# One tile more on split operands: the sixth tile's theta and the sixth step of the first mixing, in an attention and mixing kernel on one core

## The chip, the cores and the metric

The kernel runs on one core of a Trainium2 chip. The metric is device time in microseconds (us), taken from the start of the program to its end; a kernel is run several times and the median is shown. A profile is taken of one execution. Its span is the time between the first and the last instruction that the profiler saw, and the execution's own time is a little longer.

The core has five engines that run their own instruction queues in order and wait for each other through semaphores: TensorE (PE: matmuls, with its weight loads shown apart as PEld), VectorE (DVE), ScalarE (ACT), GpSimd (POOL), and SyncE (SP), which here issues every DMA.

## The reference, cut to what matters

Inputs: q, k and v of shape (4, 8, 768, 64), and four weight matrices. First a local attention with block summaries:

```python
k_sum = k.reshape(B, H, nb, 32, D).max(axis=3)
v_sum = v.reshape(B, H, nb, 32, D).mean(axis=3)
# scores of the keys within 16 positions, and of the 24 block summaries (+ log 32); one softmax over both
a = softmax([masked q k^T, q k_sum^T + log 32]);  attn = a @ [v, v_sum]
```

Then x is the attention's output as (4, 768, 512), and

```python
theta = x @ w_theta                                   # 512 x 512
zr, zi = x * cos(theta), x * sin(theta)
y = einsum('ts,bsd->btd', w_tok_r, zr) + einsum('ts,bsd->btd', w_tok_i, zi)   # 768 x 768 each
u = x + y
out = u + max(u @ w_ch, 0)
```

The weights come as 64-bit floats and are turned into 32-bit floats on the chip. All matrix products have to be good to 32-bit floats.

## The kernel before, in words

**Tiles and stages.** A batch has 768 positions, cut into six tiles of 128 positions. There are 24 tiles in all, numbered through; tiles 0 to 5 are batch 0, so "the sixth tile" is tile 5. For each tile the kernel computes the attention (`att_tile` L454: scores L490, masking with the row maximum on DVE L526, exponentials on ACT L530, transposes L539 with their copies L543, products with v L513, normalising L553 to L560); transposes the result (`turn_tile` L564: transposes L569, copy into x); computes theta and its sine and cosine (`theta_tile` L589); and multiplies to zr and zi (L631). The theta PSUM tile, `t`, has one buffer, and the transposes of `turn_tile` use the same one.

**Mixing.** For each batch there are two mixings, one for each half of the 512 channels (`mix_step` L641). One mixing has six steps, one for each tile; a step multiplies the tile's zr and zi (the stationary operands, two pieces of 128 channels each) with the rows of w_tok_r and w_tok_i that belong to the tile, and adds up in PSUM. After the sixth step DVE adds the sums to x (L678).

**The last stage.** When all batches are mixed, the channel product with w_ch is done by `out_batch` (products L775), in a scheme of seven products of half size, with sums and differences formed by DVE and POOL.

**Whole and split operands.** There are two ways to make a product that is good to 32 bits:

- whole: one matmul on 32-bit operands; the profile shows two records for it.
- split: each operand is cut into a high part in the reduced type `F32R` (`hi_op`, L289, a copy with conversion) and a low part (`lo_op`, L298, the difference), and three matmuls are made: high by high, high by low, low by high.

Two numbers decide which tiles go which way. A theta whose tile number is below `RT` is made on whole operands (L594), any other on split ones (L599). A step of the first mixing whose tile number is below `RM` is whole, any other split; the second mixing of batch 0 and all later ones are split. Both are 6 before.

```python
            if b * NT + i < K["RT"]:                                   # L593, theta_tile
        raw = b * NT + i < K["RM"]                                     # L625, theta_tile
        if t < K["RM"]:                                                # L896, after mix_step t
            for j in (2 * s, 2 * s + 1):
                split_wt(j, f_t[j])
        if j < 2 * K["RM"]:                                            # L876, weight piece j of 12
```

On split operands a tile's x is copied three times out of PSUM: whole into x, high into `xh`, low into `xl` (L571 to L577); on whole ones, once. Its z is split by `split_z` (L582). The theta weights are split (`split_f64`, L394) right ahead of the first theta that needs them. The mixing weights come in 12 pieces, j = 0 to 11, two for each step; each is turned into 32-bit floats by `to_f32` (L367 to L389, ACT, POOL and DVE). A piece of a whole step is kept as a 32-bit float, and is split after that step for the second mixing. A piece with j at or above 2 x `RM` is split at once, out of the buffer `f` (two buffers) that the conversion works in; the loads of the next batch's v (`prepass`, L435 to L440) use the same two.

**What sets the order.** Nothing is planned when the program is built: every operation (a group of instructions on one engine) has a number, in the order in which the functions register them, and the text `ORDER` lists the numbers in the order in which they are issued. A letter behind a number names the engine where several could do the work (a ScalarE, d VectorE, g GpSimd). `schedule` (L222) only reads the list. Each engine works off its own operations in that order, so an instruction that waits holds up all that stand behind it on its engine. Where DVE and POOL share work, POOL's instruction is made to wait for the DVE instruction listed just before it (the end of `attn_moe`).

## Time and profile before

| | us |
|---|---|
| median of 3 runs | 453.76 (452.31 to 454.28) |
| the profiled execution | 452.55 |
| its span | 450.8 |
| PE busy | 439.6 |
| DVE busy | 327.9 |
| ACT busy | 275.3 |
| POOL busy | 114.3 |

How to read it: a line of the profile names the source line, the engine, the operation, and the tiles it writes and reads (`m<-wt,zh` writes the mixing sums `m` and reads weights and the high part of z). Whole mixing products stand under L659 like split ones. In the chain of waits each piece has its start, its length and what it is; a piece "x24" has 24 records. In a timeline row, square brackets hold how long the engine was idle before it and what released it. A window's row gives each engine's busy time in that stretch.

### The profile page before, as it was taken

What the parts mean: (1) busy time and instruction counts of PE and PEld (TensorE: products, weight loads), DVE (VectorE), ACT (ScalarE), POOL (GpSimd) and SP (SyncE); (2) the same over time, 40 slices, a digit from 0 to 9 for tenths busy, and PEclk for the clock granted to TensorE, in tenths of its full rate; (3) what the DMA queues carried; (4) which work ended last, traced back from release to release, by engine and by line L of the source; (5) the groups of instructions that cost most, each with busy time, mean ns of one, the idle gap of its engine ahead of it and who ended that gap; (6) DMA issues with size and microseconds to landing.
All of it is one profiled execution on the core that took longest, in us unless ns stands there. A gap on an engine that the chain in (4) does not pass through costs nothing.

```text
span 450.8 us, 9379 instructions
## 1 busy us (share of the span) xinstructions
PE 439.6 (98%) x3562; PEld 358.9 (80%) x3562; DVE 327.9 (73%) x919; ACT 275.3 (61%) x579; POOL 114.3 (25%) x126
## 2 busy tenths in 40 slices
PE   7889999999999999999999999999999999999996
PEld 3455655667888888888888888888888878999996
DVE  5899999579657964666745365735646599999896
ACT  2899997787665658746684666757873123434130
POOL 3332204844251130050210100112011310114652
PEclk9999999999999999999999999999999999999999
DMA  8999965222165530405323040102005700002138
GB/s 289 358 355 333 353 185 164 90 82 70 59 224 179 151 102 22 131 19 163 101 78 106 3 117 25 55 1 76 4 0 190 278 1 0 1 1 72 53 138 300
DMA packets 24573, 55.53 MB, mean 123 GB/s; under 512 B 2768, under 2 KB 7888, under 8 KB 24528
## 3 DMA queue, kind: packets, MB, share of 16 engines
q1 hardware_dynamic: 24528, 54.93, 37.3%
q8 instruction: 28, 0.46, 0.4%
q14 instruction: 17, 0.14, 0.1%
HBM read 45.48 MB, written 9.44 MB: 122 GB/s over the span
## 4 chain that ended last, share of the span: by engine, by line
PE 90%; DMA 7%; SPq 1%; ACT 1%; DVE 0%; issue 0%; ACTq 0%
PE m L659 46%; PE t L599 11%; PE c L775 7%; PE m L775 6%; PE pa L513 5%; PE s L490 4%; PE pa L539 4%; PE t L594 3%; DMA wt<-wtr 3%; PE t L569 3%; DMA wth<-wth 2%; DMA q<-qg 2%; SPq L286 1%; PE t L775 1%; PE pa L443 0%; ACT vs L446 0%
## 5 line engine op out<-in xcount | busy, mean ns | idle before, releaser
L659 PE MATMUL m<-wt,zh 128*128 128x512 f32 (+1 forms) x768 | 179.4, 359 | 0.6 <-DVE x L678 0.6
L659 PEld LDWEIGHTS m<-wt,zh 128*128 128x128 f32 x768 | 124.0, 188 | 31.8 <-issue 12.8
L659 PE MATMUL m<-wt,zl 128*128 128x512 f32 x336 | 86.4, 338 | 0.0
L530 ACT ACTIVATE e<-e,st 128x118 f32<-128x118 f32 x192 | 62.8, 387 | 8.1 <-DVE st L526 7.6
L659 PEld LDWEIGHTS m<-wt,zl 128*128 128x128 f32 x336 | 51.5, 188 | 7.6
L526 DVE CUSTOM_DVE_ANT_0 e<-s,cs 128x118 f32<-128x118 f32 x192 | 44.4, 273 | 5.2 <-PE s L490 4.2
L599 PE MATMUL t<-wth,xh 128*128 128x512 f32 x144 | 46.7, 406 | 0.0
L610 DVE SCALAR_TENSOR_TENSOR w<-w,t 128x512 f32<-128x512 f32 x24 | 16.4, 685 | 28.5 <-ACT w L608 28.4
L301 POOL TENSOR_TENSOR zl<-zb,zh 128x512 fp32r<-128x512 f32 x16 | 21.2, 1328 | 52.5 <-DVE zh L294 24.1
L473 POOL COPY k<-kn 128x376 f32<-128x376 f32 (+1 forms) x29 | 14.0, 492 | 80.6 <-DVE zl L301 43.2
L608 ACT ACTIVATE w<-t,bmagic 128x512 f32<-128x512 f32 x24 | 16.5, 688 | 23.5 <-PE t L599 21.4
L599 PE MATMUL t<-wth,xl 128*128 128x512 f32 x72 | 28.4, 395 | 0.0
L513 PEld LDWEIGHTS pa<-v,e 118*64 118x64 f32 x768 | 24.5, 137 | 4.7 <-issue 2.5
L513 PE MATMUL pa<-v,e 118*64 118x65 f32 x768 | 27.9, 224 | 0.1
L539 PEld LDWEIGHTS pa<-cs,e 128*118 128x118 f32 x192 | 22.1, 136 | 6.3 <-issue 1.9
L490 PE MATMUL s<-k,q 64*64 64x118 f32 x768 | 25.0, 268 | 1.8 <-POOL k L473 1.8
L539 PE MATMUL pa<-cs,e 128*118 128x128 f32 x192 | 26.1, 274 | 0.3 <-ACT vs L446 0.2
L543 ACT COPY e<-pa 118x512 f32<-118x512 f32 x35 | 19.5, 586 | 10.3 <-PE pa L539 10.2
L490 PEld LDWEIGHTS s<-k,q 64*64 64x64 f32 x768 | 19.5, 132 | 7.8 <-issue 3.6
L678 DVE TENSOR_TENSOR x<-m,x 128x512 f32<-128x512 f32 (+1 forms) x32 | 16.5, 551 | 12.6 <-PE m L659 12.4
L599 PEld LDWEIGHTS t<-wth,xh 128*128 128x128 f32 x144 | 22.6, 189 | 3.4 <-issue 0.2
L543 DVE COPY e<-pa 118x512 f32<-118x512 f32 x13 | 8.9, 687 | 21.0 <-PE pa L539 21.0
(173 smaller groups left out, 790.3 us busy)
## 6 DMA issues: line engine op xcount, KB each, us to landing
v<-vg SPq DMA_DIRECT2D x48, 195.0 KB, 4.0
q<-qg SPq DMA_DIRECT2D x24, 256.0 KB, 4.4
kn<-kT SPq DMA_DIRECT2D x6, 798.0 KB, 7.6
wt<-wtr SPq DMA_DIRECT2D x6, 768.0 KB, 11.7
wt<-wti SPq DMA_DIRECT2D x6, 768.0 KB, 12.2
f<-vT SPq DMA_DIRECT2D x12, 384.0 KB, 3.9
cu<-u_scratch SPq DMA_DIRECT2D x8, 384.0 KB, 6.4
out<-cu SPq DMA_DIRECT2D x16, 192.0 KB, 2.5
```

Source lines behind the costliest of these rows:

```text
L301: lambda e: V[e].tensor_tensor(dst(), src(), hi().bitcast(F32), op=ALU.subtract), reads, writes, due, port=BOTH)
L490: mm(0.79 * len(pairs) / NP, [lambda p=p, g=g, h=h: nc.tensor.matmul(sc[h].get()[ROW[g], p], q.get()[ROW[h], p, ROW[g]], k.get()[ROW[h], p ...
L513: mm(2 * 0.433 + scores[0] + (0.2 if scores[0] else 0.0), [lambda n=n, g=g, a=a: nc.tensor.matmul(xa[a].get()[ROW[g], n], turned[a].get()[ ...
L526: op({"DVE": 0.205}, lambda eng, n=n: nc.vector.tensor_tensor_reduce(e()[:, n], sc[n % 2].get()[:, 2 * a + n // 2], mask(m), -SCALE, 3.0e3 ...
L530: op({"ACT": 0.288}, lambda eng, n=n: nc.scalar.activation(e()[:, n], e()[:, n], AF.Exp, bias=st.get()[:, n:n + 1], scale=-1.0), [(st, n)] ...
L539: mm(NH * 0.109, [lambda n=n: nc.tensor.transpose(tp.get()[:NK, n], e()[:, n], ident()) for n in range(NH)], [e_ref, (cs, "ident")], [tp], ...
L543: lambda e: (nc.scalar.copy if e == "ACT" else nc.vector.tensor_copy)(t.get()[:NK], tp.get()[:NK].rearrange("k n q -> k (n q)")), [tp], [t ...
L599: calls = [lambda t=t, xx=xx, k=k, c=c: nc.tensor.matmul(th.get(), xx.get()[:, c], w_th[c].get()[:, k], start=(c == 0 and t == 0), stop=(c ...
L608: op({"ACT": 0.59}, lambda e: nc.scalar.activation(r(), th.get(), AF.Identity, bias=bmagic.get(), scale=1.0), [th, bmagic], [R], due)
L659: nc.tensor.matmul(acc[th](), zz.get()[:, r, cc], w[:, TT[th]], start=(s == 0 and r == 0 and t == 0 and (th == 0 or c == 0)), stop=(s == N ...
L678: op({"DVE": c_dve(nt * P)}, lambda e, u=u, acc=acc: nc.vector.tensor_tensor(u(), acc(), u(), op=ALU.add), [areg] + [(xs, n) for n in rang ...
L775: calls = [lambda k=k, t=t, x=x, y=y: nc.tensor.matmul(to.get(), weights[n][x][0]()[:, k, j * P:(j + 1) * P], operands[n].get()[:, y, k], ...
```

## The change

`RT` and `RM` go from 6 to 5. So the sixth tile's theta is made on split operands instead of whole ones, and so is the sixth step of batch 0's first mixing. The weight pieces j = 10 and 11 are split as soon as they are converted, instead of being kept whole and split after the sixth step; the theta weights' split is registered ahead of the sixth tile's theta instead of the seventh's. The sixth tile gets its high and low parts of x and of z: four operations more, 1976 instead of 1972, and with them the numbers in the list shift.

The list `ORDER` is new throughout: the order of operations on all engines differs, and many operations have another engine than before. Counted over the program, DVE has 728 operations instead of 727, ACT 487 instead of 473, POOL 111 instead of 122, PE 476 and SP 174 as before.

```diff
 ORDER = """
-23 0d 11d 17g 8d 9 25 29 27 39 31 33 86 18 19 20 21 24 1d 2 3 4 5 26 30 44a 48g 49a 46a 45g 50 28 47g 51 6d 7d 52 53 60 62
+23 25 0d 1d 27 29 39 17d 15 16 2 3 4 5 31 33 86 18 19 20 21 11d 8d 9 10 14 6d 7d 24 26 44g 45g 49g 28 30 47g 46a 48a 50 51
...
-            A1=13, T1=10, PREP=5, QB=2, VSPE=1, VB=4, KB=1, WARM=5, SP0=1, FUSE=99, RELOAD=2, RT=6, RM=6, XA=6, XB=2, ZB=4, ZS=6, EB=3, TAU_A=8.2, TAU_M=4,
+            A1=13, T1=10, PREP=5, QB=2, VSPE=1, VB=4, KB=1, WARM=5, SP0=1, FUSE=99, RELOAD=2, RT=5, RM=5, XA=6, XB=2, ZB=4, ZS=6, EB=3, TAU_A=8.2, TAU_M=4,
```

More of the change, by code (lines that the diff above doesn't have):

```diff
@@ new lines @@
+52 56 189g 188g 12 60 62 55 63 53 61 54 58 87a 64 65 57 59 66 67 35 79 80a 32 34 36 37 70 68 40 183 42 93 230 100 184 186
+190 88d 38d 13 89 90 91 92g 81d 82 83 41d 84 43a 69a 71a 233a 72 191 194 193 192 199 200 201 202 73d 76d 74 77 75d 78d 22
+195 198 94a 196 204 203 197 205 206 185g 187g 234g 95g 85g 235 101a 107 283 232 231 108 109 110 111 336 96 97 102g 207 209
+218 208a 210a 236 239 287a 219a 98 103 104 238 105 211 99a 237 244 212a 118a 213 246 247 215d 243 242 250 241 245 249 248
+240 216 214d 217d 251 106g 119g 286g 120 121 220 221 222 223 252 254 224 253a 255a 288 256 285 284 225 112 404 338 337 113
@@ new lines @@
+1270 1289 1232d 1208g 1234a 1235 1271 1272a 1236a 1317 1290 1293 1255 1297 1320a 1318a 1239d 1298 1256a 1257g 1344g 1284g
+1273 1292 1296 1300 1304 1345a 1237 1238d 1301 1319 1291 1274 1275 1240 1241d 1276d 1299 1294 1295 1305 1302 1303 1261 1279
+1321 1280 1322 1333 1334 1281 1323 1308 1306 1324 1307d 1309d 1335 1346 1310 1325 1326 1327a 1328 1347 1277d 1474 1329 1331d
+1475a 1311d 1312 1332g 1477a 1476 1336 1349 1355 1358 1356 1360 1359 1348 1352 1357 1313d 1330 1337 1339 1338 1478 1340 1376
@@ new lines @@
+1479 1377 1378 1379 1374a 1384d 1314a 1350 1315 1393a 1375g 1385g 1423a 1424d 1354 1316a 1351 1394a 1353 1361 1362 1381
+1429d 1430g 1383 1380 1480 1365 1363 1481 1482 1364a 1366d 1386 1342 1390 1391 1392 1343 1435 1395 1367 1483 1529 1396 1399
+1371d 1382 1398 1404 1407 1439a 1438a 1484a 1532a 1530a 1372 1406 1531 1405 1402 1368a 1387 1388 1533 1425 1389 1534 1427
+1369 1397 1370d 1401 1403 1400 1373a 1411 1409 1410 1408 1485 1535 1412 1414 1536 1426 1440 1468d 1413d 1415d 1537 1416 1538
+1539d 1441 1449 1553 1445 1451 1443 1469d 1447 1556a 1420d 1417a 1554a 1486 1555 1428 1433 1431 1557 1434 1442 1418 1421
@@ new lines @@
+1525a 1528d 1571 1589 1613 1572 1591 1616a 1614a 1615 1617 1618 1592 1619 1611 1620 1585 1587d 1590 1609 1612 1610 1588d
+1631 1632 1629 1630 1603a 1604 1605 1607d 1608g 1633 1634 1635 1636 1586 1606 1621 1622 1623d 1624 1625 1627a 1626 1628d
+1639 1640 1641 1637d 1638d 1647d 1648d 1642 1685 1698 1686 1704 1728 1731 1692 1792 1730 1793 1795 1729 1794 1687a 1705a
+1699d 1700d 1701 1702 1688d 1706d 1689 1707 1703 1708 1690 1693a 1694g 1643 1646 1644 1709 1645 1653d 1695 1696 1697 1691
+1654d 1720a 1659a 1710d 1714a 1715d 1649 1650 1651 1652 1657 1658 1655 1663 1656 1661 1662 1660d 1667 1664 1669 1670 1665a
@@ new lines @@
+1787 1840 1818a 1820a 1836a 1857d 1813d 1811d 1824 1874 1828 1863a 1865a 1838 1839d 1845 1895 1825 1841d 1869g 1864g 1846
+1853 1849 1832 1822 1842 1826 1829 1875a 1867a 1870a 1872a 1916a 1861d 1868d 1830 1833 1866d 1876 1879 1843 1854 1897 1917g
+1850 1955 1881 1877 1878a 1884 1934 1900 1847 1880a 1871d 1896a 1851 1918d 1898 1919d 1920a 1922d 1923a 1899a 1885 1873d
+1888 1902 1901a 1909 1892 1921d 1935a 1886 1925a 1905 1926d 1882 1893 1910 1906 1936 1889 1924g 1929g 1913 1939 1941 1927a
+1937 1928d 1890 1938a 1944 1960 1903 1914 1957 1907 1834 1827 1852 1791 1767 1788 1883 1855 1780 1759 1831 1894 1784 1887
```

126 lines of the change are left out of this document (51 added, 75 removed).

## The prediction

> **What bounds the kernel now.** The page comes first: its span, the busy shares and the slices.
>
> ```profile
> span 450.8 us, 9379 instructions
> PE 439.6 (98%) x3562; PEld 358.9 (80%) x3562; DVE 327.9 (73%) x919; ACT 275.3 (61%) x579; POOL 114.3 (25%) x126
> PE   7889999999999999999999999999999999999996
> PEclk9999999999999999999999999999999999999999
> ```
>
> TensorE (PE) works in 439.6 of 450.8 us, at the full granted clock, and it is the least busy in the first three slices and the last. So the time is PE's work plus 11.2 us in which it stands still. Second, the view of waits says who held PE:
>
> ```profile
> PE t L356 <- POOL zb L354: 1.8, 1, 1.8
> PE s L490 <- POOL k L473: 1.8, 2, 1.1
> PE t L569 <- DVE w L610: 1.2, 2, 0.6
> PE t L594 <- ACT x L292: 0.8, 1, 0.8
> PE t L594 <- DVE xn L560: 0.6, 1, 0.6
> PE m L659 <- DVE x L678: 0.6, 1, 0.6
> ```
>
> The first row is the start of the program. The others come to 5.0 us, and any order could at best win these back. Third, the windows show how close the other engines are (PE, PEld, DVE, ACT, POOL, clock, DMA share):
>
> ```profile
> 40.00:80.00 40.00, 39.87 (x213) 23.22 (x214) 39.48 (x88) 36.18 (x67) 10.27 (x12) 1.00 0.75 247
> 80.00:100.00 20.00, 19.13 (x253) 13.49 (x252) 12.43 (x60) 16.19 (x38) 13.85 (x20) 1.00 0.26 78
> 363.00:448.00 85.00, 84.00 (x479) 80.43 (x479) 79.05 (x128) 27.64 (x44) 24.83 (x15) 1.00 0.20 71
> ```
>
> From 40 to 80 us VectorE (DVE) is as full as PE: 39.48 of 40 against 39.87. There two engines bound the kernel together. From 80 to 100 DVE has 7.6 us to spare, and in the last stage 5.9 of 85. The change is made inside the first two windows.
>
> **The change part by part.** *PE's own work.* The chain of waits lists PE's pieces in order (start, length, what):
>
> ```profile
> 69.59 11.75 PE m L659 x36
> ...
> 89.08 0.93 PE t L594 x2
> ...
> 91.09 2.79 PE t L594 x6
> ...
> 98.07 3.02 PE t L599 x12
> 101.09 5.16 PE m L659 x16
> ...
> 113.78 1.05 PE m L659 x6
> 114.83 0.70 PE t L599 x3
> 115.53 3.12 PE m L659 x18
> ...
> 219.33 4.23 PE m L659 x24
> ```
>
> The sixth tile's theta on whole operands is the two L594 pieces, 0.93 + 2.79 = 3.72 us. On split operands a tile's theta is the L599 row with 12 records, 3.02 us. That saves 0.70. The sixth mixing step on whole operands is the 5.16 us row (16 records); a split step is 24 records, 4.23 us. That saves 0.93. Together **-1.63 us**.
>
> By the Trainium skill (FP8 and Floating Point Precision, section TensorE Precision Notes) a true fp32 product goes through the array in four passes. If each of the three split products were one such pass, my estimate from the page would be three quarters of 3.72 and of 5.16, a saving of 2.2 us. The rows give ratios of 0.81 and 0.82, so the rows decide.
>
> *Changes between kinds of matmul.* Counted along the two written orders, PE changes kind (products of the mixings, the channel stage and whole-operand theta; theta on split operands; scores; transposes; attention products) 245 times instead of 231. Changes between the first two sorts go from 91 to 107, all others from 140 to 138. Between these two a change costs next to nothing: six records of a split step take 1.05 between two theta pieces, and 18 without a break 3.12, which is 1.04 for six. Sixteen times 0.01 is 0.2, and two of the others fall away; I take 0, with +-0.3 as bounds.
>
> *The transposes of the seventh tile.* They reuse the PSUM tile of the sixth theta, so they wait for ScalarE's rounding and DVE's subtraction of it. The timeline:
>
> ```profile
> 95.36 0.66 PE L569 MATMUL t<-cs,xn 128*128 128x128 f32 x4 [0.63 <-DVE w L610]
> ...
> 97.03 1.04 PE L490 MATMUL s<-k,q 64*64 64x118 f32 x32
> ```
>
> Between the theta and them stood only eight transposes of the attention, and PE lost 0.63. In the new order a whole block of scores (about 1 us, last row) stands there too, which is more than was missing: **-0.6 us**. (A similar wait at the third tile goes, and another of its size appears there, since that theta now follows its transposes at once; I count the two as nothing.)
>
> *What DVE gets.* Four instructions are new: the sixth tile's x and z each need a high and a low part. In the new order all four are DVE's, and the plain copy of x goes from ScalarE to DVE. The groups by form give their prices (busy, mean ns):
>
> ```profile
> L575 DVE TENSOR_TENSOR xl<-t,xh 128x512 fp32r<-128x512 f32 x18 | 12.4, 689 | 11.3 <-ACT xh L292 8.5 <-ACT x L292 1.9 <-PE pa L513 0.8
> L294 DVE COPY x<-t 128x512 f32<-128x512 f32 x10 | 6.8, 685 | 0.7 <-ACT xh L292 0.7
> L294 DVE CAST zh<-w 128x512 fp32r<-128x512 f32 x12 | 5.1, 422 | 1.9 <-PE m L659 1.8
> L301 DVE TENSOR_TENSOR wt<-wt 128x768 fp32r<-128x768 f32 x5 | 4.7, 946 | 0.0
> ```
>
> The two x parts and the copy are about 3 x 0.69, the z parts 0.42 and, a difference of the same shape as x's, 0.69: 3.2 us on DVE before the sixth step. Besides, the last two pieces of the mixing weights (rows of the sixth step) are no longer kept whole; they are split as soon as they are converted, because the two buffers they then stand in are wanted by the next batch's loads. Their low parts, 0.95 us each, now stand in DVE's queue ahead of the fifth tile's product, which the fifth step waits for. Counted along the list, 160 DVE instructions instead of 155 end with that product, 2.3 us more by durations of this trace: 1.9 for the two, the rest many small moves of both signs.
>
> Is there room for 2.3 us? The timeline shows that product:
>
> ```profile
> 75.89 0.69 DVE L631 TENSOR_TENSOR zh<-xn,w 128x512 f32<-128x512 f32 x1
> ...
> 99.78 0.69 DVE L631 TENSOR_TENSOR zh<-xn,w 128x512 f32<-128x512 f32 x1 [0.74 <-ACT w L621]
> ...
> 100.93 1.24 PE L659 MATMUL m<-wt,zh 128*128 128x512 f32 x3
> ```
>
> It ended at 76.6. The fifth step begins after 24 of the 36 records of the piece at 69.59, so at 69.59 + 11.75 x 24/36 = 77.4: slack 0.8. The stall is thus between 0 (the new order packs DVE's early queue better) and 2.3 - 0.8 = 1.5 us. With DVE at 39.48 of 40 there is little to pack, so I take the upper half: **+1.0 us**. Behind the waiting step on PE stand the seventh tile's scores and the attention of the sixth, and for these the softmax waits.
>
> *At nothing.* The theta weights' split moves ahead of the sixth tile's theta, on ScalarE, DVE and POOL, in the window where DVE has 7.6 us free. The sixth tile's chain (rounding, subtraction, sine, product, and now 0.42 + 0.69 of splitting) is hidden by PE work between theta and step: transposes, scores, attention, a held-back quarter of the fifth step and three quarters of the next theta. Without that cover its two new links would cost 1.1. SyncE issues 173 transfers before and after. In the last stage DVE gets 1.6 us more (more of the final operands' work, fewer of the accumulations), and has 5.9 free: nothing, at worst +1.6.
>
> *Sum.* The profiled execution took 452.55 us, 1.75 around its span. 452.55 - 1.63 - 0.6 + 1.0 = 451.3. The median of the runs, 453.76, is 1.21 above that execution, so against it: **452.5 us**. Bounds of this case: the DVE term 0 to 1.5, the changes of kind +-0.3, the last stage up to 1.6: 451.2 to 454.9.
>
> **The rivals.** *Faster by more:* the new order also removes early waits. If the DVE term is 0 and half of the other early waits (1.8 on POOL, 0.8 and 0.6 for theta) goes, it is 453.76 - 1.63 - 0.6 - 1.6 = **449.9**. For it: those waits are there. Against it: counted along the list, POOL's copies in front of the third tile's scores stand 1.6 us of POOL work later than before, and theta follows its transposes as closely.
>
> *Slower: DVE's queue to the sixth step.* Counted the same way, the product (now with its split) that releases the sixth step stands behind 4.0 us more DVE work than before. Before, it ended at 100.47 and the step began at 100.93. If none of the 7.6 us that DVE stands free between 80 and 100 can be used, because those gaps are waits for the exponentials and for PE, it ends at 104.5, and the step starts 3.5 late. PE's work from there on is the same within 0.2 us (the step saves 0.93, but a quarter of a theta and a little more have been put behind). That is 453.76 + 3.5 - 0.2 = **457.1**. Every microsecond of the 4.0 that the gaps take up comes off; with less than 1.0 taken up it is still over 456, and from 3.3 on it turns faster. For it: DVE's full window before, 39.48 of 40, from which it comes late. Against it: 3.2 of the 4.0 are the sixth tile's own x and z parts, and the gaps there are such as the 0.74 in front of this very product, into which work that is ready can go.
>
> *It saves nothing:* the 1.63 us of PE is saved while PE would have waited for DVE anyway, stall 1.5 and the last stage's 1.6 fully: 453.76 - 1.63 - 0.6 + 3.1 = **454.6**.
>
> *Weight loads laid bare.* A split step loads 24 weight tiles where a whole one loads 16, a split theta 12 for 8:
>
> ```profile
> L659 PEld LDWEIGHTS m<-wt,zh 128*128 128x128 f32 x768 | 124.0, 188 | 31.8 <-issue 12.8 <-DVE x L678 0.9 <-DVE zh L631 0.7
> ```
>
> If each stood in line before its matmul, 12 more at 0.188 us would add 2.3 us and the time would be 453.76 - 1.63 + 2.3 = **454.4**. But 24 loads are 4.5 us, more than the whole 4.23 us of the step that holds them, so they overlap and their price is in the rows already. The Trainium skill (TensorE: Matmul & The Clock Gate, section Part 3: Packing small matmuls) says that a weight load overlaps with a running matmul only when its row group differs; by it this rival would hold, and this trace doesn't agree.
>
> **How the numbers follow.** Forecast 0.50, faster by more 0.24, slower through DVE 0.14, saves nothing 0.11, weight loads 0.01. A change of under 0.5%, 2.3 us, can't be told from none here. Faster by over that (under 451.5): most of the faster rival, 0.20, and a fifth of the forecast, 0.10, is 0.30. Slower by over that (above 456.0): most of the slower rival and a little of the next, 0.14. Within: 0.56. The range, 449.9 to 456.4, takes in the faster rival's time and the slower one's where the gaps take up a part, and leaves out somewhat under 0.2.
>
> **What would show it.** In the profile after: PE busy about 1.6 us less; L594 with 20 + 20 records and L599 with 12 more; the sixth step at 4.2 us; no wait of the seventh tile's transposes on L610; a wait of L659 on DVE's L631 of about 1 us near 77 us, and none at the sixth step. I am wrong if PE waits over 2 us in all for DVE between 70 and 110 us, if PE's busy time doesn't fall, or if new waits of PE stand after 360 us.

## The result and the profile after

The first measurement gave 456.19 us for the changed kernel (8 runs, 454.27 to 458.37) against 453.12 for the kernel before (8 runs): ratio 1.0067, interval 1.0046 to 1.0087. Two later measurements, on two chips, gave less: 454.86, ratio 1.0029 (1.0016 to 1.0042), and 454.93, ratio 1.0028 (1.0008 to 1.0048). The kernel before, measured in the same way against itself, gave 453.63 and 0.9996 (0.9980 to 1.0011). So the change loses between 0.3% and 0.7%, about 1.3 us by the two later measurements. Three of the eight executions of the first measurement (456.90 to 458.37) had a mean granted clock of 0.996 against 0.999 to 1.0 in the other five, and one execution of the second ran at 0.755, took 542.28 and is left out. The forecast was a gain of the same size: 452.5.

The page of the profile of the changed kernel. Its execution took 455.98 us, 1.68 around the span:

```profile
span 454.3 us, 9411 instructions
PE 439.4 (97%) x3574; PEld 360.2 (79%) x3574; DVE 334.5 (74%) x920; ACT 278.0 (61%) x587; POOL 102.2 (22%) x115
PE   6888999899999999999999999999999999999996
```

PE's busy time fell by 0.2 us and not by 1.6. The span grew by 3.5, so PE stands still for 14.9 us instead of 11.2. The view of waits, changed kernel, PE alone (total, times, longest):

```profile
PE t L356 <- DVE beps L346: 1.9, 1, 1.9
PE s L490 <- DMA q<-qg: 1.6, 1, 1.6
PE t L594 <- ACT x L292: 1.4, 2, 0.7
PE pa L539 <- ACT vs L446: 1.4, 2, 0.7
PE pa L539 <- ACT e L530: 1.3, 1, 1.3
PE pa L443 <- DVE vt L439: 0.7, 1, 0.7
PE m L659 <- DVE x L678: 0.6, 1, 0.6
...
PE m L659 <- DVE zh L631: 0.2, 1, 0.2
```

The wait of the transposes on L610 is gone, as forecast. Three waits now stand in a row at the seam between the two batches' work; of the third, the view of before had 0.24. The timeline of PE, changed kernel, shows them:

```profile
81.12 2.85 PE L659 MATMUL m<-wt,zh 128*128 128x512 f32 x8 [0.24 <-DVE zh L631]
83.80 0.60 PE L539 MATMUL pa<-cs,e 128*118 128x128 f32 x4
...
85.42 0.28 PE L443 MATMUL pa<-cs,vt 128*24 128x128 f32 x1 [0.69 <-DVE vt L439]
86.38 0.65 PE L539 MATMUL pa<-cs,e 128*118 128x128 f32 x4 [0.68 <-ACT vs L446]
```

The first is the fifth step's wait for DVE that the forecast had at 1.0; it is 0.24. The other two stand around the transposes of batch 1's block means (L443, tile `vt`): DVE has not yet added up the loaded v (L439), and then ScalarE has not yet copied the result (L446). The second is not in every execution. In a second profile of the changed kernel the same transposes wait for nothing, while the 0.24 and the 0.68 are there again:

```profile
83.17 0.74 PE L443 MATMUL pa<-cs,vt 128*24 128x128 f32 x4
```

**What belongs to the execution.** The two waits of 1.6 and 1.3 belong to this execution: in the second profile of the changed kernel the same two are 0.63 and 0.25. They stand before the fourth tile's scores, while the transfers of the first 60 us are still coming in. Here are those scores in the timelines of four executions: the kernel before in its first profile, and again in a later one; then the changed kernel, twice:

```profile
30.44 1.04 PE L490 MATMUL s<-k,q 64*64 64x118 f32 x32
```

```profile
31.78 1.04 PE L490 MATMUL s<-k,q 64*64 64x118 f32 x32
```

```profile
32.61 1.04 PE L490 MATMUL s<-k,q 64*64 64x118 f32 x32
```

```profile
30.89 1.04 PE L490 MATMUL s<-k,q 64*64 64x118 f32 x32
```

The same program starts them 1.34 later in one execution than in another, and in that later one everything behind was late by 1.06 to 1.34 up to the end. Over the profiles at full clock the start lies between 0 and 2.15 behind 30.44 where the front (everything ahead of the first mixing step) is in the old order and between 0.02 and 2.41 where it is in the new one. So this lateness is no effect of the order that these runs can tell, and below, times are given net of it: a point's time, minus how late the scores began. Net of it the last product of the kernel starts 1.27 and 0.65 later than before in the two profiles of the changed kernel (1.61 in a version that differs little), which fits the 1.3 of the medians. Times net of lateness are good to about half a microsecond, no better: two profiles of one kernel differ by 0.6 here and by 0.8 for the version with the low parts moved, below. Some of the lateness also comes after the mark: the second profile waits 0.54 for a load of q at 39.5 us, where the first waits for nothing.

### The profile page after: what moved, and what is told of

It reads as the page before. It is cut to its first block, busy times and chain, and to the rows that moved or that the text cites. A ratio compares the mean times of both kernels' runs of the same rounds, so it can differ in the third digit from the quotient of the medians.

```text
span 454.3 us, 9411 instructions
## 1 busy us (share of the span) xinstructions
PE 439.4 (97%) x3574; PEld 360.2 (79%) x3574; DVE 334.5 (74%) x920; ACT 278.0 (61%) x587; POOL 102.2 (22%) x115
## 4 chain that ended last, share of the span: by engine, by line
PE 78%; DVE 10%; DMA 7%; ACT 3%; issue 1%; SPq 0%; DVEq 0%
PE m L659 39%; PE t L599 11%; PE c L775 6%; PE m L775 6%; PE pa L513 5%; PE s L490 4%; PE pa L539 3%; DMA wt<-wtr 2%; PE t L569 2%; DVE f L386 2%; DMA v<-vg 2%; DVE wt L389 2%; DMA kn<-kT 1%; ACT e L530 1%; DMA f<-vT 1%
## 5 line engine op out<-in xcount | busy, mean ns | idle before, releaser
L659 PE MATMUL m<-wt,zh 128*128 128x512 f32 (+1 forms) x768 | 178.8, 357 | 0.9 <-DVE x L678 0.6
L659 PEld LDWEIGHTS m<-wt,zh 128*128 128x128 f32 x768 | 123.5, 189 | 30.8 <-issue 10.7
L659 PE MATMUL m<-wt,zl 128*128 128x512 f32 x344 | 88.7, 339 | 0.0
L659 PEld LDWEIGHTS m<-wt,zl 128*128 128x128 f32 x344 | 52.4, 188 | 7.8
L599 PE MATMUL t<-wth,xh 128*128 128x512 f32 x152 | 49.3, 405 | 0.0
L473 POOL COPY k<-kn 128x376 f32<-128x376 f32 (+1 forms) x25 | 12.4, 506 | 84.3 <-PE s L490 23.9
L610 DVE SCALAR_TENSOR_TENSOR w<-w,t 128x512 f32<-128x512 f32 x24 | 16.4, 683 | 19.3 <-ACT w L608 19.2
L599 PE MATMUL t<-wth,xl 128*128 128x512 f32 x76 | 30.0, 394 | 0.0
L539 PE MATMUL pa<-cs,e 128*118 128x128 f32 x192 | 26.1, 274 | 3.3 <-ACT vs L446 1.4
L539 PEld LDWEIGHTS pa<-cs,e 128*118 128x118 f32 x192 | 21.8, 136 | 9.2 <-ACT e L530 2.6
L543 DVE COPY e<-pa 118x512 f32<-118x512 f32 x17 | 11.3, 687 | 22.4 <-PE pa L539 22.4
L599 PEld LDWEIGHTS t<-wth,xh 128*128 128x128 f32 x152 | 23.6, 189 | 3.5
L678 DVE TENSOR_TENSOR x<-m,x 128x256 f32<-128x256 f32 (+1 forms) x32 | 16.7, 551 | 12.9 <-PE m L659 12.9
L301 POOL TENSOR_TENSOR zl<-w,zh 128x512 fp32r<-128x512 f32 x8 | 10.9, 1361 | 64.4 <-DVE zh L294 30.6
L787 ACT COPY zb<-c 128x384 f32<-128x384 f32 x11 | 5.1, 483 | 32.8 <-PE c L775 17.7
```

The source lines that it names most:

```text
L473: lambda e: (nc.scalar.copy if e == "ACT" else V[e].tensor_copy)(dst(), src()), rd, wr, due, port=BOTH)
L539: mm(NH * 0.109, [lambda n=n: nc.tensor.transpose(tp.get()[:NK, n], e()[:, n], ident()) for n in range(NH)], [e_ref, (cs, "ident")], [tp], ...
L599: calls = [lambda t=t, xx=xx, k=k, c=c: nc.tensor.matmul(th.get(), xx.get()[:, c], w_th[c].get()[:, k], start=(c == 0 and t == 0), stop=(c ...
L610: op({"DVE": c_dve(DM)}, lambda e: nc.vector.scalar_tensor_tensor(r(), r(), MAGIC, th.get(), ALU.subtract, ALU.subtract), [th], [R], due)
L659: nc.tensor.matmul(acc[th](), zz.get()[:, r, cc], w[:, TT[th]], start=(s == 0 and r == 0 and t == 0 and (th == 0 or c == 0)), stop=(s == N ...
L678: op({"DVE": c_dve(nt * P)}, lambda e, u=u, acc=acc: nc.vector.tensor_tensor(u(), acc(), u(), op=ALU.add), [areg] + [(xs, n) for n in rang ...
```

## The experiments

All kernels compute the whole result. Numbers in the list of the order name operations; the numbers 175 and 182 are the low parts of the weight pieces 10 and 11. Three theories were tried first. **A:** the new order ahead of the first mixing step costs the time. **B:** the pieces 10 and 11, split at once, hold the two `f` buffers, so the next batch's v is loaded too late. **C:** the low parts stand too early in DVE's queue. A fourth, **K**, came later: PE's own pieces grow because other kinds of matmul now stand next to each other.

### The front alone

*The old front in the changed kernel: every operation ahead of the first mixing step in the order and on the engines of before.*

```diff
 ORDER = """
-23 25 0d 1d 27 29 39 17d 15 16 2 3 4 5 31 33 86 18 19 20 21 11d 8d 9 10 14 6d 7d 24 26 44g 45g 49g 28 30 47g
+23 0d 11d 17g 8d 9 25 29 27 39 31 33 86 18 19 20 21 24 1d 2 3 4 5 26 30 44a 48g 49a 46a 45g 50 28 47g 51 6d
...
```

> The changed kernel, with all operations that stand ahead of the first mixing step in the order of the kernel before (on the engines of before), and the rest of the list as changed. The first mixing step began 2.75 us later after the change (45.40 to 48.15). Theory A (the front of the new order is what costs): it begins near 45.4 again and the time falls by about 2.75, from 456.2 to 453.4; the wait for the last load of v near 84 us stays. Theory B (pieces 10 and 11 hold the buffers that the loads of v need): the first step is early, but the waits at 84 to 87 us grow by what was won, and the time stays at 456. Theory C (DVE has more to do ahead of the fifth and sixth step, whatever the order in front): the same, 455.5 to 456.5.

Measured: 459.14, ratio 1.012 (1.0097 to 1.0142). The first mixing step started like before (0.71 late, with scores 0.83 late), but the seam between the two orders made a wait of its own. From its timeline:

```profile
53.17 2.25 PE L490 MATMUL s<-k,q 64*64 64x118 f32 x32 [4.32 <-ACT k L473]
```

The sixth tile's k copies stood behind exponentials in ScalarE's queue. The wait costs more than its own length: from 53.2 to 59.0 us the granted clock of this profile is 0.50. This says nothing for or against A.

*The other way round: the kernel before with the new front.*

```diff
 ORDER = """
-23 0d 11d 17g 8d 9 25 29 27 39 31 33 86 18 19 20 21 24 1d 2 3 4 5 26 30 44a 48g 49a 46a 45g 50 28 47g 51 6d
+23 25 0d 1d 27 29 39 17d 15 16 2 3 4 5 31 33 86 18 19 20 21 11d 8d 9 10 14 6d 7d 24 26 44g 45g 49g 28 30 47g
...
```

> The kernel before (whole operands for the sixth tile), with only the operations ahead of the first mixing step in the order and on the engines of the changed kernel. Theory A: the first mixing step begins near 48 and the time rises by 2.75 from 453.1 to 455.9. Theories B and C: the loss belongs to the sixth tile's split, so the time stays within 0.8 of 453.1.

Measured: 455.88, 1.005 (1.0031 to 1.0068). By the medians that is 2.0 us, clear of noise, with no split in it. In its profile the first step started 3.0 and the end came 4.1 later, of which 2.41 is the execution's lateness; 1.16 of the rest is a wait behind the seam to the old order (57.16 us, the transposes of a tile for L610). So the new front costs the old kernel something; how much without the seam, this run can't say.

*The old order up to the fifth tile's products with v (operation 362), a seam at another place.* The edit is like the first of this section, only longer.

> The changed kernel with everything ahead of the fifth tile's attention products (about 55 us) in the order and on the engines of the kernel before; the seam is later than in e1, where the copies of k for the sixth tile stood behind ACT's exponentials (a wait of 4.3). Theory A (the front costs 2.0, as e2 measured): 2.0 below the changed kernel as run here, so between 1.0 below and 1.0 above the kernel before. If the new front only seems slow because DVE's work is moved between front and rest: the same as the changed kernel within 0.7.

Measured: 454.62, 1.0036 (1.0017 to 1.0056), the same as the changed kernel. The seam cost 1.62 at the fourth tile's theta, and the three waits near 80 us stayed. From its timeline:

```profile
59.34 1.12 PE L594 MATMUL t<-xh,x 128*128 128x512 f32 x2 [1.62 <-ACT x L292]
...
82.07 2.85 PE L659 MATMUL m<-wt,zh 128*128 128x512 f32 x8 [0.70 <-DVE zh L631]
```

With the old front the wait for DVE at the fifth step is even larger. The seam's 1.62 is most of the 2.0 that A would have given back, so this run doesn't settle A; one without that wait follows below.

### The buffers

*Pieces 10 and 11 are kept in the unused half of an x tile, so that `f` is free for v.* From here on, kernels with this edit have line numbers up to 6 higher behind it: L659 is L665, L631 is L637, L439 is L445, L443 is L449, L539 is L545, L473 is L479.

```diff
-        if n == S:
+        if n == S and j >= NC + 2 * K["RM"] and into is None:
+            at = (j - NC - 2 * K["RM"]) * S
+            f_ref = (spare[0], ("f", j))
+            f = lambda: spare[0].get().rearrange("p t d -> p (t d)")[:, at:at + S]
+        elif n == S:
...
-            split_wt(j, (f, (f_ref, None)))
+            split_wt(j, (f, f_ref))
```

> The changed kernel, in which the weight pieces 10 and 11 are converted and kept, until they are split, in the half of the tile x that batch 0's start no longer needs, so that the two buffers f are free for the loads of v as before. Order and engines unchanged. Theory B: the loads of v are issued from about 68 us instead of 73.6, the waits of PE at 84 to 87 us (0.69 on L439, 0.68 on L446 and what follows) go, and the time falls by 1.2 to 1.6, to 454.6 to 455.0. Theory A: the first step still begins at 48.1; if the loads were not what PE waited for, the time stays at 456.2. Theory C: 456.2.

Measured: 454.87, 1.0016 (1.0000 to 1.0033). This is the time that B forecast, but the changed kernel itself took no longer when it was measured again (454.86, below). SyncE's timeline, first the changed kernel, then this one:

```profile
73.57 1.32 SPq L286 DMA_DIRECT2D f<-vT  x2
```

```profile
61.17 0.33 SPq L286 DMA_DIRECT2D f<-vT  x1
66.03 0.33 SPq L286 DMA_DIRECT2D f<-vT  x1
```

The first two of the four loads are issued from 61.17 on instead of 73.57, and yet the same waits stand on PE, in the timeline of this kernel:

```profile
79.39 2.85 PE L665 MATMUL m<-wt,zh 128*128 128x512 f32 x8 [0.26 <-DVE zh L637]
...
83.65 0.28 PE L449 MATMUL pa<-cs,vt 128*24 128x128 f32 x1 [0.65 <-DVE vt L445]
84.61 0.65 PE L545 MATMUL pa<-cs,e 128*118 128x128 f32 x4 [0.68 <-ACT vs L452]
```

B falls: DVE comes to the sums no sooner, and the other two loads can only be issued when its first two sums have freed the buffers (77.14 here, 78.88 in the changed kernel). For the last of them DVE itself waits 0.58 here and 0.63 in the first profile of the changed kernel; in the second profile, where it doesn't, PE's wait on L443 is gone. The edit is kept in the next kernels, since it lets the low parts be moved.

*The order of the loads as before, in the changed kernel.*

```diff
-23 25 0d 1d 27 29 39 ...
+23 25 0d 1d 29 27 39 ...
...
-... 70 68 40 183 42 93 ...
+... 70 68 183 40 42 93 ...
```

> The changed kernel with the order of its loads in the front as before: q of the second tile ahead of v of the first, v of the fourth tile ahead of a further piece of the mixing weights, and two of the k loads swapped. Engines and order else unchanged. Theory A, if the loads are its cause (the wait of 0.46 for v of the fourth tile, and the first weight piece landing at 28.64 instead of 26.70): the first mixing step begins 0.7 to 2 earlier and the time falls by as much. If the loads' lateness is that of the execution: no difference to the changed kernel within 0.5.

Measured: 455.68, 1.0049 (1.0035 to 1.0064): no gain, and 0.8 more than the changed kernel on the same chip. It is not the loads' order either.

### Does the change need a new order?

*The change in the old order: the new operations put in by hand, each low part right behind its conversion.*

```diff
+... 172 168 173 174a 175d 365a 368a 329 ...
...
+... 178 179 180 181a 182d 327 379 ...
```

> The change itself (sixth tile on split operands, pieces 10 and 11 split at once) set into the old order by hand: everything ahead of the second mixing of batch 0 stands in the order of before, with the four new operations put where they are needed, the high and low parts of pieces 10 and 11 right behind their conversion, and the theta weights' split pulled ahead of the sixth tile; the rest of the list is that of the changed kernel. Theory A: the loss is in the new order's front, so this has the savings of TensorE without it, 451.5 to 452.7. Theory B: it still holds the two buffers, for a shorter time: 453 to 454. Theory C: the extra DVE work in the old order costs at least as much as in the new one, 455 to 457.

Measured: 473.8, 1.045 (1.0425 to 1.0476). From its timeline:

```profile
70.69 1.70 PE L569 MATMUL t<-cs,xn 128*128 128x128 f32 x4 [4.58 <-ACT xn L558]
...
98.98 1.63 PE L490 MATMUL s<-k,q 64*64 64x118 f32 x32 [2.44 <-POOL k L473]
...
106.19 0.70 PE L599 MATMUL t<-wth,xh 128*128 128x512 f32 x2 [2.83 <-DVE x L294]
```

The new operations don't fit where the old ones leave no gap; 20 us is the price of a careless place for them. A part of it is the clock: behind these waits it is 0.50 from 70.7 to 76.0, from 100.2 to 103.5 and from 107.0 to 110.3 us. So this run doesn't separate the change from its order.

*The changed kernel again, without an edit, on another chip than these.*

> The changed kernel itself, unaltered, beside the kernel before on the same chip as the runs it is compared with. Its first measurement was 3.05 above the kernel before (ratio 1.0067). Run e3, the same order with the two buffers f freed, was 1.0 above, but its profile still shows the waits at 83 to 85 us that theory B blamed on the buffers (0.65 on L449 and 0.68 on L452 of its own line numbers), and its gain arose before 30 us, where the two kernels are the same. If B is void, this run comes out like e3, 0.8 to 2.2 above the kernel before; if the buffers do count, it comes out 2.3 to 3.6 above.

Measured: 454.86, 1.0029 (1.0016 to 1.0042).

### DVE's queue

*The two low parts moved behind batch 1's sums.* On top of the edit of the buffers:

```diff
-... 439 440 441 442 175d 182d 379 327 389 ...
+... 439 440 441 442 379 327 389 ...
...
-... 392 398 400 499a 280g 462g 463g 464g 500g 423 424 ...
+... 392 398 400 175d 182d 499a 280g 462g 463g 464g 500g 423 424 ...
```

> Run e3's kernel (pieces 10 and 11 kept in the free half of x), in which the two low parts of those pieces stand on DVE behind the six sums for batch 1's prepass instead of ahead of them; nothing else is moved. Theory C (what stands ahead in DVE's queue sets the waits at 80 to 87 us): DVE comes to the product of the fifth tile and to the sums 1.9 earlier, the waits of 0.24 before the fifth step, 0.69 before the transposes of the sums and 0.68 behind them go, and the time is 1.2 to 1.6 below that of e3 and of the changed kernel as run here. Theory A alone: no difference to e3, within 0.4.

Measured: 458.56, 1.0116 (1.0099 to 1.0133). The waits of 0.24 and 0.69 are gone, and a larger one has come, in PE's timeline:

```profile
86.81 2.28 PE L496 MATMUL s<-k,q 64*64 64x118 f32 x32 [2.59 <-POOL k L479]
```

Here, too, the clock falls behind the wait. The window's row (PE, PEld, DVE, ACT, POOL, clock, DMA share):

```profile
86.80:92.80 6.00, 5.99 (x66) 4.41 (x67) 2.66 (x20) 2.66 (x10) 6.00 (x8) 0.50 0.28 79
```

Six microseconds of PE work at half clock cost, by my estimate from this row, about three. They belong to the 3.7 that this kernel lost on the changed one.

POOL's and DVE's timelines of the same kernel tell why:

```profile
81.75 1.82 DVE L301 TENSOR_TENSOR wt<-x,wt 128x768 fp32r<-128x768 f32 x2
...
83.71 1.86 POOL L301 TENSOR_TENSOR wt<-wt 128x768 fp32r<-128x768 f32 x1 [7.12 <-DVE wt L301]
83.82 2.29 DVE L637 TENSOR_TENSOR zb<-xn,w 128x512 f32<-128x512 f32 x1
85.51 0.81 POOL L479 COPY k<-ks 128x192 f32<-128x192 f32 x1
```

A POOL instruction is made to wait for the DVE instruction listed just before it. The low parts now stood just before POOL's next work, so POOL waited 7.12 for them, and its copies of k, which the scores need, came late. Not the length of the two was wrong, but their place relative to POOL's.

*The same two a few places further on, behind POOL's copies in the list.*

```diff
-... 392 398 400 175d 182d 499a 280g 462g 463g 464g 500g 423 424 415 ...
+... 392 398 400 499a 280g 462g 463g 464g 500g 423 424 175d 182d 415 ...
```

> As e6 (pieces 10 and 11 kept in the free half of x, their two low parts on DVE behind the sums for batch 1), but the low parts stand in the list behind the copies of k for the seventh tile and the low part that GpSimd makes there. In e6 GpSimd's first instruction there was made to wait for the two low parts, since they stood just before it in the list, and the scores of the seventh tile waited 2.59 for the copies. Theory C (DVE's queue sets the waits at 80 to 87 us): the wait of 0.24 before the fifth step and the 0.69 before the transposes of the sums go, the 2.59 of e6 goes too, and the time is 0.7 to 1.2 below e3 and the changed kernel as run again (ratio to the kernel before near 1.000). If the pair of low parts only costs wherever it stands: the same as e3, ratio 1.002 to 1.003.

Measured: 454.17, 1.0032 (1.0012 to 1.0053). Only the third of the three waits is left near 80 us, but the time is not the one that C forecast; it is that of the rival, by which the pair costs wherever it stands (1.002 to 1.003). It was measured again, beside the changed kernel on the same chip, with 12 runs each.

> Run e9's kernel again, beside the changed kernel and the kernel before on one chip. In e9's profile the waits at 80 to 84 us are gone but for one of 0.68, and from the scores of the fourth tile (start 0.96 later than before) to the end it gains 0.64 on the kernel before, where the changed kernel loses 1.26 and e3 1.58; its median was no better than theirs (ratio 1.0032). Theory C, that DVE's queue costs 1.4 to 1.9: 1.0 to 2.0 below e14 in the median. If the lateness of the first 30 us, which differs from execution to execution, covers it: within 0.8 of e14.

> The changed kernel again, for a second profile of it in an undisturbed execution and a third time. Median 1.3 to 3.0 above the kernel before. In the profile: the scores of the fourth tile between 0 and 2.4 later than before by the execution's lateness, 1.2 to 1.7 more at the end, and the same waits at 81 to 87 us (0.24, 0.69, 0.68) as in the first one.

Measured: 453.55, 1.0001 (0.9985 to 1.0016), against 454.93, 1.0028 (1.0008 to 1.0048) for the changed kernel: 1.4 us less. The wait of 0.69, which was expected again in the changed kernel, is not in its second profile. DVE's timeline, the changed kernel first, in the profile of the first measurement:

```profile
72.59 1.94 DVE L301 TENSOR_TENSOR wt<-f,wt 128x768 fp32r<-128x768 f32 x2
...
80.39 0.68 DVE L631 TENSOR_TENSOR zh<-xn,w 128x512 f32<-128x512 f32 x1
...
84.41 0.95 DVE L439 TENSOR_REDUCE vt<-f 128x24 f32<-128x768 f32 x1 [0.63 <-DMA f<-vT]
```

Then the kernel with the low parts moved:

```profile
77.81 0.68 DVE L637 TENSOR_TENSOR zh<-xn,w 128x512 f32<-128x512 f32 x1
...
81.82 0.95 DVE L445 TENSOR_REDUCE vt<-f 128x24 f32<-128x768 f32 x1 [0.61 <-DMA f<-vT]
82.69 1.94 DVE L301 TENSOR_TENSOR wt<-x,wt 128x768 fp32r<-128x768 f32 x2
```

The 1.94 us of the two low parts stand behind the fifth step's product and the sums, not ahead of them, and both end 2.6 us sooner. Of that, 0.86 is the first execution's greater lateness; the rest, 1.7, is the low parts'. PE's timeline of the second keeps one wait there:

```profile
84.27 0.66 PE L545 MATMUL pa<-cs,e 128*118 128x128 f32 x4 [0.68 <-ACT vs L452]
```

The seventh tile's scores start 1.74 and 1.67 late (net) in the profiles of the changed kernel, and 0.37 and 0.50 late in those with the low parts moved. But a part of the second profile's lateness arises between 31 and 41 us, where the two kernels are the same. PE's pieces stand in the same order in both, so they can be laid side by side from the third tile's theta (43 us) on: to the last of the transposes on L443 the low parts cost 0.65 us in the second profile, 1.35 in the first and 1.36 with the pieces kept elsewhere. About 0.4 of it is there by the fifth step each time; the rest, 0.24 to 0.96, goes with the wait on L443. So the profiles and the second measurement speak for C, the first does not; by them its size is between 0.6 and 1.4 us.

*The kernel before once more, beside these two.*

> The kernel before against itself: how far apart two measurements of one kernel lie here (ratio 1.000, within 0.001 if the chip is even), and a second profile of it: if the lateness of the first 30 us belongs to the execution, the scores of the fourth tile start at another time than 30.44, between 30.4 and 32.7, and everything behind them is late by the same amount within 0.2; if it is the new front that makes executions late, they start at 30.4 to 30.7 again.

Measured: 453.63, 0.9996 (0.9980 to 1.0011). Its profile gave the 31.78 of the section above.

### The rest: the front, the kinds, and the search for a better version

With the low parts moved, the kernel takes as long as before, though PE should have 1.6 us less to do and a wait of 0.6 is gone. Something still takes about two microseconds.

*Theory K: from operation 812 to 1569 (150 to 320 us) the order of before, on top of the moved low parts.*

```diff
-... 757 859 812 822g 823g 824 817 570 1114 ...
+... 757 859 736 892 822g 823a 812 824 570 1114 ...
...
```

> Run e9's kernel, in which the order from the first mixing of the second batch to the first mixing of the fourth (about 150 to 320 us) is that of the kernel before. TensorE waits for nothing there in either kernel, so only the neighbours of its pieces differ. Theory K (the extra TensorE time of the changed kernel, transposes 21.9 instead of 21.1 above all, comes from what stands beside them): the time of the transposes of the attention falls by 0.5 to 0.8, that of the last stage stays at 59.05 instead of 58.8, and the whole gains 0.3 to 0.8 on e13 at the same lateness. If the extra time belongs to the sixth tile's way: the transposes stay at 21.8 and the time at e13's.

Measured: 454.24, 1.0011 (0.9993 to 1.0029). The time can't tell it from the kernel without the edit. Worked out from the timeline as start to next start, summed over the program, the attention's transposes took 21.08 us before, 21.91 and 21.86 in the changed kernel, 21.78 with the low parts moved and 21.32 here. How their neighbours set this is seen in the timelines, first of the kernel before:

```profile
253.15 0.60 PE L539 MATMUL pa<-cs,e 128*118 128x128 f32 x4
253.50 0.72 PE L599 MATMUL t<-wth,xh 128*128 128x512 f32 x2
...
254.30 0.60 PE L539 MATMUL pa<-cs,e 128*118 128x128 f32 x4
254.65 0.71 PE L599 MATMUL t<-wth,xh 128*128 128x512 f32 x2
```

Then of the changed kernel, the same eight transposes:

```profile
257.22 1.03 PE L539 MATMUL pa<-cs,e 128*118 128x128 f32 x8
258.18 1.04 PE L490 MATMUL s<-k,q 64*64 64x118 f32 x32
```

Four transposes ahead of a piece of theta hold PE for 0.35, so eight for 0.70; the same eight ahead of scores hold it for 0.96. Worked out over all such groups of the two kernels, eight in a row ahead of theta take 0.79 and ahead of scores 0.97 to 0.99, so 0.2 of the difference is what comes next and 0.1 the row of eight. K's mechanism is shown, but its worth is small: with the old middle the transposes of the attention took 0.46 less and those of `turn_tile` 0.32 more, and PE's work as a whole (without the matmuls that warm it up at the start, L356) fell by 0.3 us.

*The old front once more, to operation 362, with the fourth tile's copy of x ahead of the weights' magnitudes, so that the seam makes no wait.*

```diff
-... 359a 361a 362 154a 159a 155g 323 363a ... 416 370a 324a ...
+... 359a 361a 362 370a 154a 159a 155g 363a ... 416 324a ...
```

> Run e9's kernel with everything ahead of the fifth tile's attention products in the order and on the engines of before (as e7), and the copy of the fourth tile's x ahead of two magnitudes on ACT (in e7 the theta of that tile waited 1.62 for it). Theory A in what is left of it (the new front costs 0.8 to 1.0 in waits for the copies of x): 0.8 to 1.0 faster than e13, ratio 0.997 to 0.999. If DVE, full from 30 to 80 us, sets the fifth step however the front is arranged: the waits before 55 us fall, the fifth step starts as late as in e13 at the same lateness within 0.3, and the time is e13's.

Measured: 452.91, 1.0005 (0.9987 to 1.0022). The first step starts as before (0.09 late), but PE then waits at another place, shown by its timeline:

```profile
61.98 2.85 PE L665 MATMUL m<-wt,zh 128*128 128x512 f32 x8 [1.59 <-DVE zh L637]
```

By the fifth step nothing is left of the gain: it starts 1.32 late (net), against 1.22 and 1.34 with the new front. The window from 30 to 80 us says why, this kernel's row (PE, PEld, DVE, ACT, POOL):

```profile
30.00:80.00 50.00, 47.02 (x331) 28.22 (x330) 49.64 (x117) 44.72 (x90) 14.12 (x16) 1.00 0.75 259
```

DVE has 0.36 of 50 us free. What PE gains early in this kernel it waits for DVE later, and A's 0.8 to 1.0 us don't come.

*Both: the old front and the old middle.* The two edits together.

> Both edits, of e16 and of e17, in one kernel. If both theories hold, 1.1 to 1.8 faster than e13 (ratio 0.996 to 0.998), the first version below the kernel before; if neither, e13's time (ratio 1.000).

Measured: 453.02, 0.9994 (0.9979 to 1.0010). The gain of both theories together, a ratio of 0.996 to 0.998, is not there. No version is measurably faster than the kernel before.

*Three orders searched anew for the first 760 to 800 operations, with durations from these profiles: for the change with the pieces kept elsewhere, for the change with `f`, and for the kernel before (`RT` and `RM` at 6).*

```diff
 ORDER = """
-23 25 0d 1d 27 29 39 17d 15 16 2 3 4 5 31 33 86 18 19 20 21 11d 8d 9 10 14 6d 7d 24 26 44g 45g 49g 28 30 47g
+14 8d 23 25 45a 0d 1d 27 29 31 2 39 11g 9 10 48a 86 17d 46g 3 26 28 30 18 38d 49g 4 5 19 20 47g 6d 24 7g 21
...
```

> Sixth tile split, pieces 10 and 11 in the free half of x, and the first 800 operations of the list in an order (and with engines) that was searched again with the durations and waits that the profiles of before, after and e1 to e8 show, DVE's slowing beside a GpSimd instruction among them. Theory D (the sixth tile on split operands is worth its 1.6 of TensorE, and the order in hand spends it): 2 to 4 below the changed kernel, ratio to the kernel before 0.993 to 0.998. If DVE's fuller window (39.5 of 40) leaves no order that keeps the saving: ratio 1.000 to 1.004.

> The changed kernel (pieces 10 and 11 in the two buffers f) with the first 800 operations in an order searched in the same way. Theory B in its weak form (the two buffers tie the order down): at least 0.7 slower than e10. If the buffers don't matter, as e3's waits said: within 0.6 of e10.

> The kernel before (sixth tile whole) with the first 760 operations in an order searched in the same way. Theory D: it gains less than e10, so that e10 is at least 1 faster than this one, the sixth tile's saving. If the gain of e10 is all from the order and none from the split: this one is as fast as e10 within 0.6, near ratio 0.993 to 0.998.

Measured: 458.56 (ratio 1.0123, 1.0104 to 1.0142), 464.26 (1.0242, 1.0224 to 1.0261) and 460.31 (1.0154, 1.0139 to 1.0168). All lose. Among themselves they stand as the theories had it (with `f` 5.7 slower, the sixth tile whole 1.75 slower), but each is the find of another search, so this can't be put down to the buffers or to the split. The search had put more on POOL. Windows and groups by form, first of the kernel before, then of the first of the three:

```profile
30.00:80.00 50.00, 48.56 (x334) 28.91 (x333) 49.41 (x117) 45.54 (x89) 12.82 (x15) 1.00 0.81 262
```

```profile
L631 DVE TENSOR_TENSOR zb<-xn,w 128x512 f32<-128x512 f32 x5 | 3.4, 693 | 0.0
```

```profile
30.00:80.00 50.00, 44.03 (x319) 25.58 (x318) 48.37 (x113) 42.31 (x83) 23.07 (x21) 1.00 0.75 253
```

```profile
L637 DVE TENSOR_TENSOR zb<-xn,w 128x512 f32<-128x512 f32 x5 | 5.2, 1037 | 0.0
```

With POOL busy for 23.07 instead of 12.82 us, the same DVE product takes 1037 ns instead of 693 (the groups are those of the first 100 us). PE is busy for 4.5 us less in the window. In the other two POOL is busy for 20.10 and 19.01 us there, but this product stays at 703 and 698; in all three the weights' conversion on DVE (L389, here L393) takes 1071, 1071 and 1030 instead of 961. The search did reckon with DVE's slowing beside POOL, so what it missed, and how much of the 5 to 11 us is DVE's slowing, no run shows.

## Why the prediction was wrong, by its steps

The net loss of 1.3 us against the 1.2 us gained in the forecast is 2.5 us to account for. The account is made from profiles net of lateness, averaged over the two of the changed kernel and that with the pieces kept elsewhere, against the two of the kernel before; its terms are good to about half a microsecond.

- **PE's own work, -1.63: right.** The chain of waits, changed kernel:

```profile
93.94 3.00 PE t L599 x12
...
104.06 4.23 PE m L659 x24
```

  The step gives 4.23 for 5.16, and theta 3.0 for 3.72 (start to next start 2.93 for 3.70, so -1.70 in all).

- **Changes between kinds, 0 +-0.3: wrong, about +0.7.** This is the first failed step. PE's busy time without the warming matmuls went from 432.3 to 432.0 instead of down by 1.7, so 1.3 are missing. With the low parts moved, and PE's pieces in the same order, it is 431.2 and 431.5: 0.6 of the 1.3 is no matter of neighbours and belongs to DVE's queue (the first five steps took 26.30 before, 26.54 in the changed kernel and 26.27 with the low parts moved). For the other 0.7, start to next start, the attention's transposes took 0.8 more and the last stage 0.3 (58.77 to 59.10), the transposes of `turn_tile` 0.24 less, and smaller pieces a little of both. I had counted changes of kind, which hardly rose; what counts is which kind stands next. That this made the whole 0.7 is not shown: the one run that put back the neighbours, from 150 to 320 us, gave back 0.3 of PE's work and no time that 12 runs resolve. The condition "if PE's busy time doesn't fall" named this, and it all but came true: it fell by 0.2 to 0.3.

- **The seventh tile's transposes, -0.6: right.** No wait on L610 is left in the changed kernel's list, where before there were two of 0.6. The pair in brackets held as well: at the third tile the 0.60 on L610 went, and a wait of its theta for the copy of x came, 0.74 and 0.68 in the two profiles.

- **DVE's queue, +1.0: mechanism right, place in part wrong, size 0.6 to 1.4.** The two low parts did stand ahead of too much; moving them alone gives back 1.4 us by the medians of the second measurement and 0.65 to 1.36 by the profiles laid side by side. At the fifth step, where the forecast had the stall, PE waited only 0.24 and lost 0.4 in all. The rest came behind: the sums of batch 1's v, which the prediction did not follow, stand behind the same low parts, and in the first profile their transposes wait 0.69 for them, in the second not at all. (The 0.68 after these is there with the low parts moved too; it isn't theirs.) The forecast asked what DVE delays first, and not what it delays next.

- **The waits that have no term in the sum: wrong, about +1.4.** This is the second failed step. Outside PE's work the time grew by 1.5 net of lateness (the program's start included); less the -0.6 for the transposes and the 0.7 of DVE's queue that shows as standing still, 1.4 remain. No run isolated them; the list of waits shows where they lie. Behind the fourth tile's scores the two profiles of the changed kernel have 0.58 and 0.61 for a normalised result ahead of the fifth tile's attention (L558), 0.46 and 0.56 for a load of v, and 0.68 for the copy of batch 1's means, which took 0.24 before; the second has 0.54 for a load of q besides. The view of waits in the forecast stopped short of its last two rows, 0.3 and 0.2, and the last is this very copy (L446). The wait for v is in seven of the nine profiles with the new front (0.21 to 0.86) and in none with the old one. The old front does away with those for v and for the normalised result, but in the run with it DVE then holds the second step for 1.59. In this window PE and DVE bound the kernel together, as the prediction's first part said, and a new order there can't be left out of the sum.

- **At nothing.** No wait of PE on the sixth tile's chain or on the theta weights is found; PE's waits after 360 us are as before: 0.6 on L678, quoted in both lists.

```profile
366.40:451.40 85.00, 84.37 (x479) 80.72 (x479) 78.61 (x126) 28.65 (x49) 19.20 (x13) 1.00 0.20 71
```

  This is the last stage of the changed kernel; the window begins 3.4 us later than the forecast's, since the stage ends so much later. DVE is busy for 78.61 instead of 79.05, so the 1.6 more that the forecast had counted for it are not seen. The terms at nothing held.

- **The rivals.** "Slower through DVE's queue to the sixth step" did not happen: no wait stands at the sixth step, and the gaps between 80 and 100 us took the work up (DVE is busy for 15.74 of these 20 us in the changed kernel, 12.43 before). "Faster by more" fell with its condition: the DVE term was not 0. "It saves nothing" came near in time, 454.6 against 454.9, but not for its reason; the 1.6 of the last stage isn't there. "Weight loads laid bare" falls: the step with 24 loads takes 4.23. That the measured times lie inside the range is luck: its upper part was there for a stall at the sixth step, and none came.

The sum as it came out: -1.7 (PE) -0.6 (L610) +1.4 (DVE, of which 0.6 shows as PE's work) +0.7 (neighbours, in part shown) +1.4 (other waits, a remainder) = +1.2, which is what these profiles lost, against +1.3 measured twice. The DVE term alone has an experiment behind it that gives time back; with its lower bound, 0.6, the last two would be larger by 0.8 together. What stays open: why the loss was 1.7 us larger by the ratio of the first measurement than by the two later ones. The executions at the lower clock are a part of it at most: without them the median falls from 456.19 to 455.79. Its profile was late by 2.17 at the fourth tile's scores, more than most, but no run shows what makes a run late there.

## What to carry to other kernels

When an instruction is put into a full queue, follow everything behind it until the first real gap, and not only the first consumer that waits: here the second one cost more in one of two executions. Count what a matmul costs from its start to the next one's start in its own neighbourhood. A new order is a change of its own: here it brought waits of about 1.4 us that no term of the sum had. Where two engines are both full, a saving on one is no saving until the other has been given room.

## What was not expected of the hardware

**DVE waits beside POOL.** The DVE product of 0.69 us took 2.29 in the run shown above, started 0.11 after a POOL subtraction of 1.86, and ended 0.54 after POOL's end at 85.57: a little less than its own length later. POOL's own instruction took hardly longer than others of its kind (1.81 to 1.83). By the Trainium skill (SBUF — State Buffer, section Who interferes with whom) a DVE instruction with two inputs in SBUF contends with a POOL instruction that reads SBUF, for ports that one of them at a time holds alone. If POOL holds them to its end, my estimate is 1.75 of waiting and 0.69 of work, 2.4, and the trace agrees within 0.2. In the first searched order four of the five products met a POOL instruction (0.76, 1.13, 1.31 and 1.31 us, the fifth 0.68), and the mean rose from 693 to 1037 ns.

**The early transfers are late by as much as the change was worth.** The same program reached its fourth tile's scores 1.34 us apart in two executions, and the kernels here spread over 2.4 us. One profile of each kernel would have put 2.2 us to the change that are not its own.

**A wait of PE can cost its clock as well.** Behind PE's waits of 2.59, 4.32 and 4.58 us in three of these runs the granted clock was 0.50 for several microseconds, as the windows above say. Not the length alone decides: in the run with the change in the old order the clock was also 0.50 behind a wait of 2.44, and in the first searched order it stayed at 1.00 behind one of 2.49.
